# Linear attention and two MLPs on one core: who issues the weights' raw bits from unit 7 on

## The chip, the core and the metric

The kernel runs on one core of a Trainium2 chip. The metric is the device time of one execution in microseconds, as a median over several. TensorE does the matmuls, VectorE and ScalarE the elementwise work, GpSimd little else than memsets here. Any engine's instruction stream can start transfers between DRAM and SBUF; in this kernel nearly all are started by SyncE's (SP). Whatever stream starts them, they are carried out by the core's 16 DMA engines.

## The reference, cut to what matters

```python
def _attn_ref(q, k, v):            # 4 batches, 8 heads, 576 positions, 64 wide
    q_s = softmax(q, axis=-1)      # over the 64
    k_s = softmax(k, axis=2)       # over the 576
    kv = np.einsum('bhsd,bhse->bhde', k_s, v)
    return np.einsum('bhsd,bhde->bhse', q_s, kv)

x = attn_out.transpose(0, 2, 1, 3).reshape(2304, 512)
# first MLP: w_in 512 x 2048, w_out 2048 x 512
r = np.maximum(x @ w_in, 0.0)
x = (s * (r * r) + b) @ w_out
# second MLP, same sizes
h = x @ w_in2
out = (h * np.tanh(softplus(h))) @ w_out2
```

The two softmaxes and softplus are written out in the reference; they are shortened here. The weights of both MLPs reach the kernel as 64-bit floats.

## The kernel before, in words

**Stages.** Attention and the first MLP run interleaved in a loop of 80 steps: 5 chunks of tokens (512, 256, 512, 512, 512), each with 16 blocks of 128 hidden columns. Step n computes h of step n + 2 (`emit_h`, w_in times x), its activation (`emit_relu2`: ScalarE's Relu L222 and Square L223, a cast to a high part gh, and VectorE's low part gl, L175), and y of step n (`emit_y`, w_out times g). Every product is done in three passes of high and low parts (L185). The second MLP follows from about 470 us and is not touched.

**The first MLP's weights** come in 17 units. Units 0 and 1 hold one block of w_in, units 2 to 15 block f of w_in and block f - 2 of w_out, unit 16 the last two blocks of w_out. A block's raw bits are one transfer of 512 KB (`load_raw`, L116 for w_in, L121 for w_out); `load_w` issues a unit's two. They are turned into 32-bit floats by ScalarE's Abs (L133) and four passes on VectorE (L141, L145, L150, L155), and split into a high part (ScalarE, L164) and a low part (VectorE, L175), which take the place of the raw bits in the unit's slot.

**Slots.** Each unit has a slot of its own in SBUF, but some slots hold attention's data first: those of units 8 to 11 chunk 0's q of head pairs 0 to 3 (later also ke and km of batch 0), those of units 12 to 15 k, v and the block-diagonal kv of batch 0 (`kvb0` to `kvb3`, with `bd` in it). A raw load into such a slot waits until its last reader is done. For units 12 to 15 that is `kv_lo` of head pair 0 to 3 (VectorE's kvl, L175), which runs in chunk 1's part of the table below. The q of chunk 0 is loaded from ScalarE's stream; k, v and later q from SP's. Batches 1 to 3 share one buffer for k (`kb`) and one for v (`vb`), so each head pair's load waits for the one before to be used (k by VectorE's ke, L443; v by TensorE's kv, L487).

**Order.** A table (`at`, `run`) says in which step each load, conversion or attention stage is recorded. Raw bits of units 0 to 6 are recorded ahead of the loop (`early`), those of unit u from 7 on at the end of step u - 7; its high and low parts at step u - 3. What each engine then executes is decided by a scheduler, which simulates the recorded program and reorders each engine's instructions. So a different issuer for a transfer gives other orders on other engines as well. In the names below, `raw0_7` is the raw tile of unit 7, `t0_7` its converted copy, `w0_7` its high and low parts, `km1_0` the maximum of k for batch 1 and head pair 0, and `gl12` the low part of the activation of step 12.

The lines that decide which units the change touches:

```python
    for i in range(NU):
        u, s = (0, i), i - 3
        ...
        if s >= 4:
            at(s - 4, "load", load_w, *u)
        else:
            early.append((s, u))
```

Of the kernel before, what the change touches and what calls it, by code (L numbers as in the profile page):

```python
# [17 lines left out]
P = 128  # L18
# [9 lines left out]
def kernel(  # L28
# [21 lines left out]
    nc = tc.nc  # L50
    B, H, S, D = q.shape
    NT, DM = out.shape
# [56 lines left out]
    def slot(i, name, dt=F32):  # L109
        wp = next(pool for _, pool, last in wps if i <= last)  # L110
        return wp.tile([P, (2 if i < 2 else 4) * DM], dt, tag=f"w{i}", name=name)

    def load_raw(ph, z, f, part):
        src = srcs[ph, z].bitcast(I32)
        if z == "wi":
            nc.sync.dma_start(  # L116
                out=part.rearrange("p (k f) -> p k f", k=NK),
                in_=src[:, 2 * f * P:2 * (f + 1) * P].rearrange("(k p) f -> p k f", p=P),
            )
        else:  # L120
            nc.sync.dma_start(out=part, in_=src[f * P:(f + 1) * P, :])  # L121

    def load_w(ph, u):
        raw = slot(u, f"raw{ph}_{u}", I32)
        for i, (z, f) in enumerate(UNITS[u]):
            load_raw(ph, z, f, raw[:, 2 * i * DM:2 * (i + 1) * DM])
        w_raw[ph, u] = raw[:, 0:2 * len(UNITS[u]) * DM].rearrange("p (n w) -> p n w", w=2)

    def conv_abs(ph, u):
# [125 lines left out]
    def prep_load(z, i, pool):  # L255
        r = [pool.tile([P, 2 * DM], I32, tag="t", name=f"r{j}_{z}{i}") for j in range(2)]
        for j in range(2):
            load_raw(1, z, i + j * NF // 2, r[j])
        t, s = (pool.tile([P, 2 * DM], F32, tag="t", name=f"{a}_{z}{i}") for a in "ts")
        prep[z, i] = (r, t, s)  # L260
# [329 lines left out]
    def at(slot, what, fn, *args):  # L590
        todo.setdefault((slot, what), []).append((fn, args))
# [6 lines left out]
    for c in range(1, NC):  # L598
        wide = CHUNKS[c - 1] == CM
        for hp in range(NP):  # L600
            s = (c - 1) * NF + 3 * hp - (c > 1)
# [24 lines left out]
    for i in range(NU):  # L626
        u, s = (0, i), i - 3
        if s > 0:
            at(s - 1, "abs", conv_abs, *u)
            at(s - 1, "bits", conv_bits, u)  # L630
        if s >= 0:
            at(s, "hi", conv_hi, *u)
            at(s, "lo", conv_lo, *u)
        if s >= 4:
            at(s - 4, "load", load_w, *u)
        else:
            early.append((s, u))
    early.sort()
# [12 lines left out]
    for i in range(NF // 2):  # L651
        s = (17, 24, 31, 35, 39, 43, 47, 51)[i]
# [4 lines left out]
        s = (55, 59, 62, 63, 66, 67, 70, 71)[i]  # L657
# [7 lines left out]
    for hp in range(NP):  # L665
# [4 lines left out]
        if hp:  # L670
            v_load(0, hp - 1)
    load_w(*early[0][1])
    v_load(0, NP - 1)
    bds.append(ap.tile([P, P], F32, name="bd"))
# [3 lines left out]
    for _, u in early[1:4]:  # L678
        load_w(*u)
# [66 lines left out]
    for n in range(NS):  # L746
        ph, c, f = steps[n]
# [180 lines left out]
```

## Time and profile before

| | us |
|---|---|
| median of 3 runs | 857.91 |
| lowest and highest of them | 857.65, 861.57 |
| the profiled execution's own time | 858.7 |
| its span in the profile | 856.9 |
| TensorE, matmuls busy | 824.0 |
| VectorE busy | 630.5 |
| ScalarE busy | 495.9 |
| GpSimd busy | 3.7 |

The span runs from the first instruction to the last; the 1.8 us that the execution takes beyond it lie around it. The mean granted clock of TensorE was 0.994 of its full speed. Busy times of engines overlap one another, so they don't add up to the span. The times of rows come from the one profiled execution; the median comes from the others.

### The profile page before, as it was taken

How to read it: one execution, taken by the hardware profiler on the slowest of the kernel's cores; microseconds unless marked ns; L12 is line 12 of the kernel's file. 1: busy time of each engine (PE TensorE's matmuls, PEld its weight loads, DVE VectorE, ACT ScalarE, POOL GpSimd, SP SyncE). 2: the span in 40 equal slices, each digit the busy share in tenths (PEclk: the TensorE clock that was granted, in tenths of full speed). 3: DMA queues.
4: the chain of work that ended last, by engine and by line, in shares of the span. 5: the costliest groups of instructions: out<-in, count | busy, mean ns of one | idle time of the engine just before them, and what ended most of it. 6: DMA issues, size and time to landing. Idle time of an engine off the chain costs nothing.

```text
span 856.9 us, 14204 instructions
## 1 busy us (share of the span) xinstructions
PE 824.0 (96%) x5060; PEld 739.0 (86%) x5060; DVE 630.5 (74%) x1190; ACT 495.9 (58%) x1109; POOL 3.7 (0%) x26
## 2 busy tenths in 40 slices
PE   6798998999899999999999999999999999999998
PEld 4377877998678888888888699999999999999998
DVE  6999876576665657778685868776877858878764
ACT  7777675587666666646655744455444447244542
POOL 1000000000000000000000000000000000000000
PEclk9999999999999999999999999999999999999999
DMA  8992231566666314455797497888887888888882
GB/s 232 310 328 66 81 92 52 155 202 173 195 205 185 113 44 134 167 194 175 267 333 259 157 357 253 268 266 266 304 278 250 279 259 307 288 251 265 256 266 80
DMA packets 130150, 184.44 MB, mean 215 GB/s; under 512 B 43552, under 2 KB 94240, under 8 KB 130080
## 3 DMA queue, kind: packets, MB, share of 16 engines
q1 hardware_dynamic: 128992, 182.49, 66.4%
q10 hardware_dynamic: 1088, 1.05, 0.4%
q8 instruction: 40, 0.66, 0.3%
q14 instruction: 30, 0.25, 0.1%
HBM read 140.51 MB, written 42.99 MB: 214 GB/s over the span
## 4 chain that ended last, share of the span: by engine, by line
PE 73%; DVE 11%; DMA 9%; ACT 3%; SPq 2%; issue 2%; DVEq 0%; ACTq 0%
PE p L185 37%; PE y L185 17%; PE h L185 16%; DMA kb<-in_k_dram 2%; DMA raw<-in_moe_w_out_dram 2%; DMA xf<-yd 2%; DVE t L155 2%; DVE t L150 1%; PE x L185 1%; DVE xo L175 1%; DVE gl L175 1%; DVE w L175 1%; DVE t L288 1%; DMA r_wo<-in_moe_w_out_dram 1%; ACT xf L726 1%
## 5 line engine op out<-in xcount | busy, mean ns | idle before, releaser
L185 PE MATMUL h<-xh,w 128*128 128x512 f32 (+1 forms) x640 | 199.4, 376 | 10.1 <-ACT w L164 5.2
L185 PE MATMUL y<-gh,w 128*128 128x512 f32 (+1 forms) x640 | 196.0, 371 | 2.7 <-ACT gh L178 2.6
L185 PE MATMUL p<-ring,op 128*128 128x256 f32 x1512 | 183.0, 283 | 0.5 <-DVE op L175 0.3
L185 PEld LDWEIGHTS p<-ring,op 128*128 128x128 f32 x1512 | 182.4, 192 | 0.9 <-DVE op L175 0.9
L185 PE MATMUL p<-xo,ring 128*128 128x384 f32 x1008 | 175.9, 334 | 0.0
L185 PEld LDWEIGHTS p<-xo,ring 128*128 128x128 f32 x1008 | 174.6, 188 | 0.1
L185 PEld LDWEIGHTS h<-xh,w 128*128 128x128 f32 x640 | 118.0, 190 | 33.5 <-ACT w L164 6.0
L185 PEld LDWEIGHTS y<-gh,w 128*128 128x128 f32 x640 | 117.0, 189 | 23.0 <-ACT gh L178 3.7
L185 PE MATMUL y<-gl,w 128*128 128x512 f32 (+1 forms) x320 | 119.1, 375 | 6.0 <-DVE gl L175 5.9
L185 PE MATMUL h<-xl,w 128*128 128x512 f32 (+1 forms) x320 | 120.1, 376 | 0.0
L820 ACT ACTIVATE g<-g 128x384 f32<-128x384 f32 x96 | 50.5, 526 | 111.2 <-DVE g L288 111.1
L178 ACT CAST op<-g 128x384 fp32r<-128x384 f32 x144 | 72.8, 512 | 46.5 <-PE p L185 45.7
L175 DVE TENSOR_TENSOR op<-g,op 128x384 fp32r<-128x384 f32 x144 | 79.1, 555 | 24.2 <-ACT op L178 24.0
L175 DVE TENSOR_TENSOR gl<-r,gh 128x512 fp32r<-128x512 f32 (+1 forms) x80 | 50.7, 634 | 48.1 <-ACT gh L178 48.1
L288 DVE TENSOR_TENSOR u<-u,p 128x384 f32<-128x384 f32 (+1 forms) x117 | 57.4, 500 | 29.7 <-PE p L185 29.3
L185 PEld LDWEIGHTS y<-gl,w 128*128 128x128 f32 x320 | 60.6, 189 | 19.1 <-DVE gl L175 9.2
L222 ACT ACTIVATE r<-h 128x512 f32<-128x512 f32 (+1 forms) x80 | 44.2, 553 | 45.9 <-DVE gl L175 24.2
L185 PEld LDWEIGHTS h<-xl,w 128*128 128x128 f32 x320 | 60.9, 190 | 10.7 <-DVE xl L175 0.6
L288 DVE TENSOR_TENSOR g<-u,p 128x384 f32<-128x384 f32 x96 | 53.2, 554 | 15.1 <-PE p L185 11.8
L452 ACT ACTIVATE q<-q,qm 128x64 f32<-128x64 f32 x144 | 48.1, 337 | 12.9 <-DVE qm L433 12.7
L223 ACT ACTIVATE r<-r 128x512 f32<-128x512 f32 (+1 forms) x80 | 47.1, 588 | 1.6
L178 ACT CAST gh<-r 128x512 fp32r<-128x512 f32 (+1 forms) x80 | 46.0, 575 | 1.4
(127 smaller groups left out, 825.6 us busy)
## 6 DMA issues: line engine op xcount, KB each, us to landing
ring<-wo_d SPq DMA_DIRECT2D x84, 512.0 KB, 4.7
ring<-wi_d SPq DMA_DIRECT2D x72, 512.0 KB, 4.8
raw<-in_moe_w_in_dram SPq DMA_DIRECT2D x16, 512.0 KB, 5.9
raw<-in_moe_w_out_dram SPq DMA_DIRECT2D x16, 512.0 KB, 7.1
r_wi<-in_moe_w_in_dram SPq DMA_DIRECT2D x16, 512.0 KB, 5.7
wi_d<-r_wi SPq DMA_DIRECT2D x16, 512.0 KB, 3.0
r_wo<-in_moe_w_out_dram SPq DMA_DIRECT2D x16, 512.0 KB, 5.9
wo_d<-r_wo SPq DMA_DIRECT2D x16, 512.0 KB, 3.0
```

The source lines that it names most:

```text
L150: nc.vector.scalar_tensor_tensor(out=w_t[u], in0=w_raw[u][:, :, 1], scalar=-0x40000000, in1=w_t[u], op0=ALU.bitwise_and, op1=ALU.bitwise_or,)
L155: nc.vector.scalar_tensor_tensor(out=w_t[u], in0=w_raw[u][:, :, 0], scalar=29, in1=w_t[u], op0=ALU.logical_shift_right, op1=ALU.bitwise_or,)
L175: eng.tensor_tensor(out=lo, in0=src, in1=hi.bitcast(F32), op=ALU.subtract)
L178: nc.scalar.copy(out=hi, in_=src)
L185: mm = nc.tensor.matmul(out=ps, lhsT=x, rhs=y, start=start, stop=stop)
L222: nc.scalar.activation(out=r, in_=h_ps.pop(m), func=AF.Relu)
L223: nc.scalar.activation(out=r, in_=r, func=AF.Square)
L288: nc.vector.tensor_tensor(out=out, in0=a, in1=b, op=op)
L452: nc.scalar.activation(out=t[:, i // rq, i % rq], in_=t[:, i // rq, i % rq], func=AF.Exp, bias=mx[:, i], accum_out=sm[:, i])
L726: nc.scalar.activation(out=t, in_=t, func=AF.Identity, bias=bsum[:, kk:kk + 1])
L820: nc.scalar.activation(out=t, in_=t, func=AF.Mish)
```

## The change

`load_raw` and `load_w` are told which engine's stream to issue on, with SP's as the default. The loop's table passes GpSimd's for units 7 to 16: 20 transfers. Units 0 to 6 and all loads of attention and of the second MLP stay where they were.

```diff
--- before.py
+++ after.py
@@ -110,20 +110,20 @@
         wp = next(pool for _, pool, last in wps if i <= last)
         return wp.tile([P, (2 if i < 2 else 4) * DM], dt, tag=f"w{i}", name=name)
 
-    def load_raw(ph, z, f, part):
+    def load_raw(ph, z, f, part, eng=nc.sync):
         src = srcs[ph, z].bitcast(I32)
         if z == "wi":
-            nc.sync.dma_start(
+            eng.dma_start(
                 out=part.rearrange("p (k f) -> p k f", k=NK),
                 in_=src[:, 2 * f * P:2 * (f + 1) * P].rearrange("(k p) f -> p k f", p=P),
             )
         else:
-            nc.sync.dma_start(out=part, in_=src[f * P:(f + 1) * P, :])
-
-    def load_w(ph, u):
+            eng.dma_start(out=part, in_=src[f * P:(f + 1) * P, :])
+
+    def load_w(ph, u, eng=nc.sync):
         raw = slot(u, f"raw{ph}_{u}", I32)
         for i, (z, f) in enumerate(UNITS[u]):
-            load_raw(ph, z, f, raw[:, 2 * i * DM:2 * (i + 1) * DM])
+            load_raw(ph, z, f, raw[:, 2 * i * DM:2 * (i + 1) * DM], eng)
         w_raw[ph, u] = raw[:, 0:2 * len(UNITS[u]) * DM].rearrange("p (n w) -> p n w", w=2)
 
     def conv_abs(ph, u):
@@ -632,7 +632,7 @@
             at(s, "hi", conv_hi, *u)
             at(s, "lo", conv_lo, *u)
         if s >= 4:
-            at(s - 4, "load", load_w, *u)
+            at(s - 4, "load", load_w, *u, nc.gpsimd)
         else:
             early.append((s, u))
     early.sort()
```

Since the order of the engines' streams is the scheduler's, three places are shown where it differs.

The first is GpSimd's stream in the first microseconds, as a piece of the difference (a + is a row that is only in the changed kernel). The memsets prepare attention's tiles: `kb` and `vb` of the later batches, `kvb1` to `kvb3` of batch 0.

```order
 L354 MEMSET vb_116 128x10
 L677 MEMSET kb_115 64x2x64
+L116 DMA raw0_7_554<-in_moe_w_in_dram 128x4x256
+L121 DMA raw0_7_554<-in_moe_w_out_dram 128x1024
+L121 DMA raw0_16_1158<-in_moe_w_out_dram 128x1024 x2
 L355 MEMSET kvb1_130 64x130
 L355 MEMSET kvb2_142 64x130
 L355 MEMSET kvb3_154 64x130
 L355 MEMSET vb_116 64x130
+L116 DMA raw0_8_611<-in_moe_w_in_dram 128x4x256
+L121 DMA raw0_8_611<-in_moe_w_out_dram 128x1024
+L116 DMA raw0_9_663<-in_moe_w_in_dram 128x4x256
```

The loads of units 7 and 16 now stand among the memsets, ahead of four of them; units 8 and 9 follow, then 12, 10, 11, 13, 14 and 15. On SP's stream these 20 rows are gone.

The second place is VectorE's stream where unit 2 is converted. `xl0_0_3` is the low part of chunk 0's last x block, `t0_3` to `t0_5` belong to units 3 to 5, and `qs1_0` and `q1_0` to chunk 1's q. Before:

```order
L155 SCALAR_TENSOR_TENSOR t0_2_438<-raw0_2_180,t0_2_438 128x1024
L463 TENSOR_SCALAR qs1_0_558<-qs1_0_558 128x4
L150 SCALAR_TENSOR_TENSOR t0_3_447<-raw0_3_183,t0_3_447 128x1024
L141 TENSOR_SCALAR t0_4_493<-t0_4_493 128x1024
L464 RECIPROCAL qs1_0_558<-qs1_0_558 128x4
L141 TENSOR_SCALAR t0_5_563<-t0_5_563 128x1024
L175 TENSOR_TENSOR xl0_0_3_417<-x0_3_414,xh0_0_3_416 128x512
L425 TENSOR_REDUCE km1_0_523<-km1_0_525 128x1
L155 SCALAR_TENSOR_TENSOR t0_3_447<-raw0_3_183,t0_3_447 128x1024
L145 TENSOR_SCALAR t0_4_493<-t0_4_493 128x1024
L467 TENSOR_TENSOR q1_0_190<-q1_0_190,qs1_0_558 128x2x2x64
L175 TENSOR_TENSOR w0_2_444<-t0_2_438,w0_2_444 128x1024
```

In the changed kernel, from the same first low part of x on:

```order
L175 TENSOR_TENSOR xl0_0_3_417<-x0_3_414,xh0_0_3_416 128x512
L150 SCALAR_TENSOR_TENSOR t0_2_438<-raw0_2_180,t0_2_438 128x1024
L410 TENSOR_TENSOR km1_0_523<-kb_115 128x2x2x64
L141 TENSOR_SCALAR t0_3_447<-t0_3_447 128x1024
L155 SCALAR_TENSOR_TENSOR t0_2_438<-raw0_2_180,t0_2_438 128x1024
L425 TENSOR_REDUCE km1_0_523<-km1_0_525 128x1
L145 TENSOR_SCALAR t0_3_447<-t0_3_447 128x1024
L175 TENSOR_TENSOR gl0_480<-r0_481,gh0_479 128x512
L427 TENSOR_SCALAR km1_0_523<-ident_90,km1_0_523 128x128
L150 SCALAR_TENSOR_TENSOR t0_3_447<-raw0_3_183,t0_3_447 128x1024
L175 TENSOR_TENSOR w0_2_444<-t0_2_438,w0_2_444 128x1024
```

In the changed kernel unit 2's last two passes (L150 and L155) stand behind that low part of x, with the first rows of `km1_0` (L410, L425, L427, whose input is batch 1's k) and the first gl among them; rows of units 4 and 5 that stood ahead of unit 2's low part (the last row of both) stand behind it.

The third place is VectorE's stream where `kvl0_3` is made, the last reader of the slot of unit 15. `gl12`, `gl13` and `gl14` are low parts of activations, `qtl1_2` that of chunk 1's transposed q, `rs1_2` sums of batch 1. Before:

```order
L175 TENSOR_TENSOR w0_14_1225<-t0_14_1169,w0_14_1225 128x1024
L433 TENSOR_REDUCE qm2_0_1466<-q2_0_1382 128x8
L175 TENSOR_TENSOR kvl1_2_1125<-bd_173,kvh1_2_1124 128x128
L175 TENSOR_TENSOR kvl0_3_1253<-kvb3_154,kvh0_3_1252 128x128
L175 TENSOR_TENSOR gl12_1192<-r12_1193,gh12_1191 128x512
L425 TENSOR_REDUCE km1_3_1131<-km1_3_1133 128x1
L427 TENSOR_SCALAR km1_3_1131<-ident_90,km1_3_1131 128x128
```

In the changed kernel:

```order
L175 TENSOR_TENSOR w0_14_1225<-t0_14_1169,w0_14_1225 128x1024
L512 TENSOR_SCALAR rs1_2_1119<-kv1_2_1085 128x1
L515 RECIPROCAL rs1_2_1119<-rs1_2_1119 128x1
L175 TENSOR_TENSOR gl13_1246<-r13_1247,gh13_1245 128x512
L175 TENSOR_TENSOR qtl1_2_1128<-qt1_2_1096,qth1_2_1127 128x256
L175 TENSOR_TENSOR kvl1_2_1125<-bd_173,kvh1_2_1124 128x128
L175 TENSOR_TENSOR kvl0_3_1253<-kvb3_154,kvh0_3_1252 128x128
L425 TENSOR_REDUCE km1_3_1131<-km1_3_1133 128x1
L427 TENSOR_SCALAR km1_3_1131<-ident_90,km1_3_1131 128x128
L175 TENSOR_TENSOR gl14_1305<-r14_1306,gh14_1304 128x512
```

Before, `kvl0_3` stands ahead of `gl12`; in the changed kernel it stands behind `gl13`, which depends on h of step 13.

## Rows read from the trace of the kernel before

**Rows 1.** The page: span, and part 1, busy time by engine
```profile
span 856.9 us, 14204 instructions
...
PE 824.0 (96%) x5060; PEld 739.0 (86%) x5060; DVE 630.5 (74%) x1190; ACT 495.9 (58%) x1109; POOL 3.7 (0%) x26
```

**Rows 2.** TensorE's waits, whole run: us in total, times, longest us
```profile
PE y L185 <- DVE gl L175: 5.9, 7, 1.9
PE h L185 <- ACT w L164: 5.2, 3, 3.7
...
PE km L419 <- DVE km L410: 1.1, 1, 1.1
...
PE km L428 <- DVE km L427: 0.9, 1, 0.9
```

**Rows 3.** Busy us by stretch: PE, PEld, DVE, ACT, POOL; then clock, DMA, GB/s
```profile
10.00:15.00 5.00, 3.96 (x32) 2.88 (x32) 4.72 (x15) 4.76 (x23) 0.00 (x0) 1.00 0.76 169
...
20.00:25.00 5.00, 4.95 (x39) 2.41 (x40) 4.83 (x13) 4.67 (x11) 0.00 (x0) 1.00 1.06 369
25.00:30.00 5.00, 3.50 (x29) 1.76 (x24) 4.96 (x13) 4.70 (x8) 0.00 (x0) 1.00 0.63 177
40.00:100.00 60.00, 54.80 (x278) 42.78 (x277) 60.00 (x87) 43.99 (x82) 0.00 (x0) 1.00 0.51 164
```

**Rows 4.** The chain in order of time, 100 to 135 us
```profile
114.33 1.06 ACT w L164
...
117.23 0.41 DVE kvl L175 x2
...
118.12 4.71 DMA raw<-in_moe_w_out_dram
...
130.83 1.05 ACT w L164
...
131.93 1.22 PE h L185 x2
```

**Rows 5.** TensorE's timeline, 115 to 133 us
```profile
117.88 0.47 PE L185 MATMUL h<-xh,w 128*128 128x512 f32 x1
...
127.06 0.80 PE L487 MATMUL kv<-vb,ke 128*64 128x65 f32 x20
127.80 0.44 PE L496 MATMUL qt<-ident,q 128*128 128x128 f32 x2
```

**Rows 6.** GpSimd's timeline, 0 to 15 us
```profile
4.08 0.20 POOL L677 MEMSET kb<- 64x128 f32 x1
```

**Rows 7.** Timelines: TensorE's from 12.5 us, SP's from 35 us
```profile
12.88 1.35 PE L487 MATMUL kv<-kvb,q 128*64 128x65 f32 x20
...
36.02 0.60 SPq L116 DMA_DIRECT2D raw<-in_moe_w_in_dram  x1
...
40.92 0.46 SPq L116 DMA_DIRECT2D raw<-in_moe_w_in_dram  x1
```

**Rows 8.** Transfers: the chain; the raw tiles; the page's DMA issues (KB, us)
```profile
20.85 8.40 DMA kb<-in_k_dram
...
DMA to landing us min/median/max: 3.9/6.5/12.1
...
raw<-in_moe_w_out_dram SPq DMA_DIRECT2D x16, 512.0 KB, 7.1
```

**Rows 9.** VectorE's conversion: its timeline, and the chain
```profile
41.55 1.22 DVE L175 TENSOR_TENSOR w<-t,w 128x1024 fp32r<-128x1024 f32 x1
...
50.38 0.60 DVE t L141
50.98 1.14 DVE t L155
```

**Rows 10.** The page, part 5: ScalarE's costliest groups of MLP1's activation
```profile
L222 ACT ACTIVATE r<-h 128x512 f32<-128x512 f32 (+1 forms) x80 | 44.2, 553 | 45.9 <-DVE gl L175 24.2
...
L223 ACT ACTIVATE r<-r 128x512 f32<-128x512 f32 (+1 forms) x80 | 47.1, 588 | 1.6
L178 ACT CAST gh<-r 128x512 fp32r<-128x512 f32 (+1 forms) x80 | 46.0, 575 | 1.4
```

## Prediction

> **What bounds the kernel now.** I read the page first. TensorE is busy for 824.0 of 856.9 us [rows 1], so a change can win at most some 33 us, and only where TensorE waits. The list of TensorE's waits says where. For gl, the low part of an MLP activation that VectorE makes, it waits 5.9 us in seven places; for ScalarE's high part of a weight unit 5.2 us in three places, of which one is 3.7 us; for km of attention's second batch 1.1 and 0.9 us [rows 2]. The table by stretches says why. VectorE is busy for all 60 us from 40 to 100: it converts the weights, and no work on it can be late there without TensorE feeling it. The 16 DMA engines are full early (a share of 1.06 from 20 to 25 us); 10 to 15 us with 0.76 and 25 to 30 us with 0.63 have room [rows 3]. So the start (0 to 45 us) hangs on transfers, the middle on VectorE, and from about 130 us TensorE itself is the bound.
>
> The 3.7 us is one chain, and it is the one that the change touches. kv_lo of head pair 3 (second of the two kvl at 117.23) frees the slot that raw bits of unit 15 go into; SP then issues them, they land at 122.8, ScalarE's Abs and VectorE's bits follow, and the high part ends at 131.88; the h matmul of unit 15 begins at 131.93 [rows 4]. From the kvl's end (117.64) to that matmul are 14.3 us. TensorE had ended h of unit 13 at 118.35, and its own work was done at 128.24 [rows 5]: 9.9 us of work against 13.6 us of chain, so 3.7 us of waiting.
>
> **What the change moves.** Twenty transfers of 512 KB (units 7 to 16, some 10 MB) leave SP's queue for GpSimd's. Nothing is added or removed in computation. Four consequences, each costed alone.
>
> 1. SP's time. SP loses 20 issues of 0.4 to 0.6 us, and its waits for slots of units 8 to 15. Behind those waits stood k, v and q of chunk 1. k has one buffer, though, and its next load still waits for VectorE's ke; TensorE's waits that name this km are 1.1 and 0.9 us, each in one place [rows 2]. I cost the gain at 0, bounds 0 and -2.0.
>
> 2. The start. GpSimd's last memset ahead of its first new issue begins at 4.08 us [rows 6], so units 7 and 16 (2.1 MB) are asked for then and not from 36 us on; unit 8 follows when head pair 0's q slot is free (its kv matmuls end at 14.2 us) and not at 40.92; unit 9 behind it [rows 7]. SP needs the same engines for attention's first k and v, raw of units 0 to 3 and k of chunk 1. 1.05 MB at the 369 GB/s of the busiest early stretch takes 2.85 us [rows 3]. Units 7 and 16 cost 5.7 us, less the 1.2 us of room from 10 to 15 us; 8 costs 2.85 and 9 about half, less its room: some 9 us in front of k of chunk 1, which landed at 29.25 [rows 8], so at about 38. On VectorE's new order this k (km of head pair 0) stands ahead of the second half of unit 2 (rows of the order above). From 38.2: km 0.33, unit 3's first step 0.6, unit 2's last step 1.13, then 0.4 + 0.6 + 0.6 + 0.2 + 1.13 for the rows between, and unit 2's low part 1.13 by [rows 9] for 1024 elements (0.60 for tensor_scalar, 1.13 for the others) and by size for the smaller ones: 44.3. Before, that low part ended at 42.8. That is 1.5 us late, with no delay added for the order of the queues; since VectorE has no idle time behind it until 100 us, I carry 2 us to TensorE. Lower bound: all of this hidden. Then the new order, which puts some 3 us of units 3 to 5 behind unit 2's low part, gives 3 us back. Upper bound: the whole 11.4 us of units 7, 16, 8 and 9 land on the path, less 3.5 us of gl waits that would be absorbed: 8. Range -3 to +8, taken +2, since the nearest row (1.06) says that the engines have little room.
>
> 3. Unit 15. The order decides here. Before, the two kvl stand ahead of gl of step 12; in the changed kernel they stand behind gl of step 13. That gl needs h of unit 13, and so ReLU 0.55, Square 0.59 and cast 0.58 [rows 10]; ahead of the kvl come five small ones of ScalarE (cast of q, two copies into bd, two casts), at most 0.57 each by the same rows and by their size an estimate of 2.0 together, and 0.4 for the pair itself [rows 4]. It ends some 4.1 us behind the end of h of unit 13; gl lies under ScalarE's part. Before, it was 0.7 us ahead of it. TensorE's work between that end and h of unit 15 grows too, because kv and q's transpose of head pair 2 (0.80 and 0.44, as pair 3's [rows 5]), its x products and km's transposes now stand there: to the 9.9 us of before come 1.2 and an estimate of 1.8 for the twelve small matmuls: 12.9 us. So 4.1 + 14.3 - 12.9 = 5.5 us of waiting against 3.7: +1.8 if GpSimd's transfer lands as fast as SP's did (4.7 us from the second issue). No transfer of before goes by GpSimd. Bounds: as SP's here, 0; or the slowest of the 32 raw transfers, 12.1 us from issue to landing, 7.4 us more [rows 8]. I take 1.3, half the way to the 7.1 us that is the median of the w_out ones. Term: +3.1, bounds +1.8 and +9.2.
>
> 4. Units 7 to 14 have cover: unit 14's high part ended at 115.4 [rows 4], when TensorE still had h of unit 13 to end and y of step 11 ahead of it [rows 5], and its kvl now stands ahead of gl of step 9, as before. The four memsets that now queue behind four of GpSimd's issues are needed first by kv of head pair 1, which comes behind pair 0's end at 14.2 us [rows 7]: four issues of 2.5 us would still be hidden. Cost 0.
>
> Against its own execution of 858.7 us: 858.7 + 2 + 3.1 = 863.8. That execution lies 0.8 us above the median of 857.91, so **863 us**.
>
> A rule of the Trainium skill speaks against the change. The page "SBUF — State Buffer", section "SBUF: two separate sides", says that a DMA issued from GpSimd has its descriptors written by GpSimd's cores, and that they are locked out while VectorE runs an operation in a 2-port mode. VectorE's rows show an f32 tensor_scalar on 1024 elements at 0.60 us beside 1.13 for the two-input forms [rows 9], which fits such a mode; that GpSimd is held up no run here shows. By the rule the sum would go up by a share of a VectorE operation for each issue on the path, to the fourth rival below.
>
> **The rivals.**
> - *Hidden start, same end* (within 0.5%): the early loads find enough room and unit 15 waits only 1.8 us more. 857.9 - 1 + 1.8 = 858.7; with the start at +1, 860.7. For it: 37% of the engines' time from 25 to 30 us is free. Against: the full engines ahead of it.
> - *Faster*: the rewritten order. gl stands ahead of conversion work in many more places, and the 5.9 us of gl waits go [rows 2], and the start gives its 3 us; with unit 15 at +1.8 that is 857.9 - 5.9 - 3 + 1.8 = 850.8. It decides if k of chunk 1 lands by about 34 us, so that unit 2's low part ends by 40.
> - *Much slower*: GpSimd's issues are slow among VectorE's work. If each of unit 15's two transfers takes 2.5 us longer, and the early ones push the whole 11.4 us in front of units 0 to 3, it is 857.9 + 8 + 3 + 3 = about 872. By the page above, this is where the lock would lead; for it speaks VectorE's 60 of 60 us [rows 3].
> - *No effect at all* can be left out: the order shows every one of the twenty on GpSimd's queue.
>
> By another page of the Trainium skill, "DMA: Bandwidth & Descriptors", section "Issuing engines are not separate DMA queues", issuing from more engines saves only the issue time, as all transfers share the 16 engines. That is the first consequence at its bound and the second at its cost; by it alone the time would be 860 and more.
>
> **How the numbers follow.** 863 as summed (861.5 to 867): 0.38. Much slower (867 to 875): 0.16. Within 4.3 us of 857.9, which is 0.5% and about what a measurement of this kernel can tell from no change: 0.33, of which most lies above 857. Faster by more: 0.13. The sum stands just outside the 0.5%, so part of its own range falls to "same"; I give faster 0.14, same 0.34, slower 0.52. The range that leaves out no more than 2 in 10 is 854 to 871: it takes in the hidden start and most of the gl gain below, and the start's upper bound with unit 15 at +3 above.
>
> **What would show it.** In the changed kernel's profile: raw of units 7 and 16 landing before 20 us; k of chunk 1 landing near 38; VectorE idle in short pieces between 20 and 40 us; y of step 0 starting near 45 and not 42.8; a wait of TensorE of 5 us or more (in one or two pieces, at kv of head pair 3 and at h of unit 15) around 132 us. I am wrong if VectorE shows no idle time before 45 us (then the start is free), if the kvl of head pair 3 runs before h of unit 13 ends (then unit 15 is no loss), or if the waits for gl are gone between 55 and 85 us (then it is faster).

## The result and the profile after

The changed kernel takes 872.25 us (median of 4 runs, 871.35 to 872.44) and the kernel before 859.28 us beside it (857.65 to 861.57): 13.0 us more, a ratio of 1.0147 with a 95% interval of 1.0118 to 1.0176. The forecast was 863, range 854 to 871: slower, as said, but more than twice as much so, and 1.3 us outside the range.

The page of the profiled execution answers to [rows 1]:

```profile
span 870.3 us, 14225 instructions
...
PE 827.6 (95%) x5060; PEld 743.1 (85%) x5060; DVE 630.5 (72%) x1190; ACT 496.0 (57%) x1109; POOL 16.4 (2%) x46
```

The span grew by 13.4 us. TensorE's busy time grew by 3.6 us with the same 5060 matmuls, so 9.8 us are idle time. Where they lie, the table by stretches shows: the stretch and its length; busy time (and rows) of TensorE, its weight loads, VectorE, ScalarE and GpSimd; then granted clock, DMA share and GB/s. First the kernel before, then the changed one:

```profile
0.00:40.00 40.00, 27.53 (x165) 17.35 (x166) 31.03 (x71) 30.55 (x104) 3.70 (x26) 0.96 0.91 265
40.00:60.00 20.00, 17.41 (x90) 12.95 (x88) 20.00 (x30) 15.61 (x29) 0.00 (x0) 1.00 1.06 368
60.00:140.00 80.00, 73.70 (x387) 59.26 (x388) 67.71 (x107) 55.70 (x124) 0.00 (x0) 0.98 0.29 79
140.00:200.00 60.00, 58.86 (x517) 55.89 (x516) 38.03 (x84) 41.77 (x118) 0.00 (x0) 1.00 0.58 171
200.00:300.00 100.00, 95.50 (x522) 77.63 (x521) 62.96 (x125) 65.39 (x174) 0.00 (x0) 0.98 0.55 166
```

```profile
0.00:40.00 40.00, 22.04 (x145) 14.10 (x145) 21.25 (x54) 23.02 (x88) 12.55 (x40) 0.95 1.01 318
40.00:60.00 20.00, 14.45 (x48) 11.34 (x49) 15.02 (x24) 12.77 (x24) 0.00 (x0) 0.68 0.87 273
60.00:140.00 80.00, 76.14 (x397) 61.38 (x395) 68.37 (x106) 54.62 (x104) 3.84 (x6) 0.98 0.23 66
140.00:200.00 60.00, 53.33 (x414) 48.75 (x415) 38.18 (x77) 39.12 (x116) 0.00 (x0) 0.94 0.45 131
200.00:300.00 100.00, 98.30 (x606) 81.86 (x605) 66.39 (x136) 71.77 (x203) 0.00 (x0) 1.00 0.58 175
```

Subtracting busy time from each stretch, idle time is 5.5 us more from 0 to 40 us, 3.0 more from 40 to 60, 3.1 more from 60 to 200 (2.4 less up to 140, 5.5 more behind it), and 2.8 less from 200 to 300; the rest, to the end, is 1.1 more. So the start carries 8.5 of the 9.8 us. In the second stretch the mean granted clock is 0.68 of full speed where it was 1.00, after TensorE's longest wait (7.17 us, up to 43.59), so part of the stretch ran at the lower of the two levels, 1.2 GHz (0.50 from 40 to 48 us). h's matmuls kept TensorE busy for 0.36 us each in it (9.97 us for 28), before for 0.25 (9.36 for 38): for 28 of them that is 3.1 us, most of the 3.6 that were added to the busy time.

What the start waits for is shown by ScalarE's Abs of units 1, 2 and 3 on its timeline (in brackets the idle time ahead and what ended it):

```profile
33.30 0.66 ACT L133 ACTIVATE t<-raw 128x512 f32<-128x512 f32 x1 [2.21 <-DMA raw<-in_moe_w_in_dram]
...
41.91 1.12 ACT L133 ACTIVATE t<-raw 128x1024 f32<-128x1024 f32 x1 [6.67 <-DMA raw<-in_moe_w_out_dram]
...
45.45 1.19 ACT L133 ACTIVATE t<-raw 128x1024 f32<-128x1024 f32 x1 [1.31 <-DMA raw<-in_moe_w_out_dram]
```

Before, these three began at 23.54, 24.73 and 27.57 us. All three wait for SP's transfers, which the change did not touch. The chain of the changed kernel has unit 2's second transfer in it:

```profile
24.12 17.70 DMA raw<-in_moe_w_out_dram
...
42.92 0.62 ACT w L164
...
43.59 5.93 PE h L185 x13
```

Before, SP had issued it at 17.29 us. GpSimd's timeline up to 35 us says what was beside it:

```profile
4.22 0.90 POOL L116 DMA_DIRECT2D raw<-in_moe_w_in_dram  x1
5.11 1.57 POOL L121 DMA_DIRECT2D raw<-in_moe_w_out_dram  x3
...
16.74 0.76 POOL L116 DMA_DIRECT2D raw<-in_moe_w_in_dram  x1 [9.40 <-DVE q L410]
17.50 0.53 POOL L121 DMA_DIRECT2D raw<-in_moe_w_out_dram  x1
20.97 0.76 POOL L116 DMA_DIRECT2D raw<-in_moe_w_in_dram  x1 [2.94 <-issue]
...
22.74 0.76 POOL L116 DMA_DIRECT2D raw<-in_moe_w_in_dram  x1 [0.49 <-PE kv L487]
...
24.78 0.76 POOL L116 DMA_DIRECT2D raw<-in_moe_w_in_dram  x1 [0.77 <-issue]
...
31.81 0.76 POOL L116 DMA_DIRECT2D raw<-in_moe_w_in_dram  x1 [5.75 <-ACT w L164]
```

That is units 7 and 16, then 8, 9, 12, 10 and 11: 12 transfers by 26.1 us and 14 by 33.1, some 7.3 MB. In 40 us the engines moved 318 GB/s where they had moved 265 (12.7 MB, not 10.6). So 2.1 MB of the 7.3 were extra and about 5.2 MB pushed out others: at the 376 GB/s of the busiest five microseconds (35 to 40 us) that is, as an estimate, 14 us of transfers. From 20 to 35 us the table of DMA queues shows it directly (packets, MB, share of the 16 engines; then issues, KB each, median us to landing). `q0` is GpSimd's queue (10.49 MB in the whole run, its 20 loads), `q1` SP's:

```profile
q0 software_dynamic: 995, 3.62, 67.1%
q1 hardware_dynamic: 2641, 1.65, 38.4%
...
raw<-in_moe_w_in_dram POOLq DMA_DIRECT2D x4, 512.0 KB, 9.8
raw<-in_moe_w_out_dram POOLq DMA_DIRECT2D x4, 512.0 KB, 10.8
raw<-in_moe_w_in_dram SPq DMA_DIRECT2D x3, 512.0 KB, 17.8
raw<-in_moe_w_out_dram SPq DMA_DIRECT2D x2, 512.0 KB, 18.7
```

In the kernel before, the same stretch had `q1` alone:

```profile
q1 hardware_dynamic: 3884, 4.39, 89.1%
```

In the raw tiles' view the issue itself tells the same (ns, least, median, most):

```profile
L121 POOL DMA_DIRECT2D raw<-in_moe_w_out_dram x11: 528/528/531, 5.1 to 134.0; - x11
L116 POOL DMA_DIRECT2D raw<-in_moe_w_in_dram x9: 761/761/895, 4.2 to 133.3; - x9
...
L121 SPq DMA_DIRECT2D raw<-in_moe_w_out_dram x5: 502/599/6203, 24.1 to 48.8; - x5
...
DMA to landing us min/median/max: 4.1/7.5/19.8
```

GpSimd's issues take 0.53 or 0.76 us here (the first 0.90), and over the whole run its transfers land in 6.1 and 7.4 us (medians for w_in and w_out; SP's were 5.9 and 7.1 before). It is SP's that suffer most: one of its issues took 6.2 us, and the slowest raw transfer, SP's for unit 3, 19.8 us against 12.1 [rows 8].

### The profile page after: what moved, and what is told of

Same layout as the page of the kernel before. It is cut to its first block, busy times and chain, and to the rows that moved or that the text cites. A ratio compares the mean times of both kernels' runs of the same rounds, so it can differ in the third digit from the quotient of the medians.

```text
span 870.3 us, 14225 instructions
## 1 busy us (share of the span) xinstructions
PE 827.6 (95%) x5060; PEld 743.1 (85%) x5060; DVE 630.5 (72%) x1190; ACT 496.0 (57%) x1109; POOL 16.4 (2%) x46
## 3 DMA queue, kind: packets, MB, share of 16 engines
q0 software_dynamic: 2880, 10.49, 3.5%
## 4 chain that ended last, share of the span: by engine, by line
PE 77%; DVE 8%; DMA 8%; ACT 3%; SPq 2%; issue 2%; POOL 0%; DVEq 0%; ACTq 0%; POOLq 0%
PE p L185 36%; PE h L185 19%; PE y L185 19%; DMA raw<-in_moe_w_out_dram 2%; DMA xf<-yd 2%; PE x L185 1%; DMA kvb<-in_v_dram 1%; DMA kb<-in_k_dram 1%; DVE xo L175 1%; DVE op L175 1%; DMA q<-in_q_dram 1%; DVE t L288 1%; ACT q L452 1%; PE kv L487 1%; PE qt L496 1%
## 5 line engine op out<-in xcount | busy, mean ns | idle before, releaser
L185 PE MATMUL h<-xh,w 128*128 128x512 f32 (+1 forms) x640 | 200.3, 378 | 13.6 <-ACT w L164 12.7
L185 PEld LDWEIGHTS h<-xh,w 128*128 128x128 f32 x640 | 118.4, 191 | 36.3 <-ACT w L164 14.3
L185 PEld LDWEIGHTS y<-gl,w 128*128 128x128 f32 x320 | 61.6, 192 | 13.5 <-DVE gl L175 3.3
L185 PEld LDWEIGHTS h<-xl,w 128*128 128x128 f32 x320 | 61.4, 192 | 10.6 <-DVE xl L175 0.7
```

The costliest lines, as they stand in the source:

```text
L185: mm = nc.tensor.matmul(out=ps, lhsT=x, rhs=y, start=start, stop=stop)
```

## The experiments

Theory A: GpSimd's loads start early and crowd out, on the shared DMA engines, what is needed sooner. Rivals: it is GpSimd's own way of issuing (B), or the late slot of unit 15 (C). Two more came up on the way, on the gain of the versions without early loads: SP's queue set free (D), or the order and the moment of the loads, whoever issues (E).

Each version gets an order of its own from the scheduler, and the versions ran on several chips. The ratio is to the kernel before, run beside each on the same chip (its medians there are 858.99 to 860.36 us). Beside the median the table gives two places in each version's profile, found by counting twelve matmuls a step on TensorE's timeline: the start of h of step 3, which the transfers of the start set, and the start of y of step 68, near the end of the first MLP.

| version | early transfers on the second queue, by 35 us | h, step 3 | y, step 68 | median | ratio (95% interval) |
|---|---|---|---|---|---|
| before | 0 | 48.45 | 435.93 | 859.28 | 1 |
| changed | 14 | 59.86 | 447.84 | 872.25 | 1.0147 (1.0118 to 1.0176) |
| e1, held until unit 6 has landed | 0 | 51.08 | 429.27 | 847.05 | 0.9857 (0.9824 to 0.9889) |
| e2, only 7 and 16 | 4 | 49.52 | 427.07 | 849.78 | 0.9888 (0.9855 to 0.9922) |
| e3, 8 to 15 | 10 | 52.17 | 445.98 | 869.91 | 1.0110 (1.0070 to 1.0151) |
| e4, before and 12 unread | 12 | 53.87 | 448.25 | 873.97 | 1.0173 (1.0125 to 1.0222) |
| e5, changed, kvl early | 17 | 67.25 | 449.38 | 871.65 | 1.0122 (1.0099 to 1.0145) |
| e6, only 8 to 11 | 8 | 52.74 | 438.74 | 860.21 | 0.9994 (0.9977 to 1.0011) |
| e7, changed, ScalarE issues | 12 | 60.58 | 448.07 | 875.23 | 1.0169 (1.0139 to 1.0199) |
| e8, held until unit 3 has landed | 8, from 28.9 on | 51.01 | 447.48 | 868.91 | 1.0096 (1.0077 to 1.0115) |
| e9, before and 4 unread | 4 | 49.86 | 436.42 | 861.37 | 1.0012 (0.9993 to 1.0031) |
| e10, only 12 to 15 | 2 | 50.77 | 437.73 | 859.16 | 0.9998 (0.9969 to 1.0027) |
| e11, e1 with kvl early | 0 | 47.74 | 426.79 | 849.71 | 0.9894 (0.9854 to 0.9934) |
| e12, 7 and 16 free, 8 to 15 held | 4 | 48.46 | 430.32 | 849.79 | 0.9882 (0.9861 to 0.9903) |
| e13, e1 with SP as issuer | 0 | 48.88 | 429.11 | 849.71 | 0.9909 (0.9876 to 0.9942) |
| e14, e1 again | 0 | 51.76 | 429.45 | 849.47 | 0.9884 (0.9865 to 0.9903) |

**Hold the loads back (e1).** GpSimd copies two values of unit 6's raw bits into a small tile, and from there into each raw slot, so its transfers wait for unit 6. The computation is unchanged.

```diff
+    gate = const.tile([P, 2], I32, name="gate")
...
         raw = slot(u, f"raw{ph}_{u}", I32)
+        if u >= 7:
+            nc.gpsimd.tensor_copy(out=raw.rearrange("p (h w) -> p h w", h=2)[:, :, 0], in_=gate)
...
+    nc.gpsimd.tensor_copy(out=gate, in_=w_raw[0, 6].rearrange("p (h n) w -> p h n w", h=2)[:, :, 0, 0])
     for hp in range(NP):
```

> The changed kernel, but GpSimd copies one column of the raw bits of unit 6 into a small tile and from there into each raw slot of units 7 to 16, so that none of its 20 transfers starts before unit 6 has landed. Theory A (early bytes: the start is late because GpSimd asks for 12 transfers of 512 KB ahead of 33 us, which share the DMA engines with attention's first loads and units 1 to 3): h of step 3 starts within 2 us of the 48.45 us of the kernel before, not at 59.9, and the time is 857 to 863 us. Theory B (GpSimd's issue is slow, or held up while VectorE works): nothing is mended, 868 us or more. Theory C (unit 15's slot comes free late): the wait near unit 15 stays, about 3 us, and the start as in A: 861 to 864 us.

It took 847.05 us: not only is the loss gone, it is 10 us below A's range, and so faster than the kernel before by more than the early loads explain (D and E, below). GpSimd's first raw transfer starts at 43.68 us, step 3 is 2.6 us late, and the stretches from 0 to 40 and 40 to 60 us have TensorE busy for 26.48 and 17.55 us, nearly the 27.53 and 17.41 of before. Still all 20 are GpSimd's, so theory B falls. The wait for high parts is 1.2 us in the whole run, so C's 3 us are not there. (The expectations say 12 transfers ahead of 33 us; the timeline has 14.)

**Take the units apart (e2, e3, e6, e10).** One line of the changed kernel's table decides who issues which unit:

```diff
-            at(s - 4, "load", load_w, *u, nc.gpsimd)
+            at(s - 4, "load", load_w, *u, nc.gpsimd if i in (7, 16) else nc.sync)
```

e3 has `i not in (7, 16)`, e6 `8 <= i <= 11` and e10 `12 <= i <= 15`.

> Only units 7 and 16 on GpSimd (4 transfers, asked for from about 4 us on), 8 to 15 stay on SP. Theory A: a third of the early bytes, all of them in front of attention's first k and v: h of step 0 about 4 us late (31 us and not 26.5), h of step 3 some 4 to 6 us late, 862 to 866 us. Theory B: the few issues of GpSimd meet no VectorE work at 4 us, 858 to 860 us. Theory C: no loss, since unit 15 is issued by SP: 858 to 860 us.

> Units 8 to 15 on GpSimd, 7 and 16 back on SP. Theory A: the early bytes are 8 transfers from about 16 us on instead of 12 from 4 us on: h of step 0 on time (26.5 us), h of step 3 some 6 to 8 us late, 865 to 869 us. Theory B: nearly as the changed kernel, 870 to 873 us. Theory C: the whole loss is unit 15's, 870 to 873 us.

> Only units 8 to 11 on GpSimd, which wait for the slots of chunk 0's q. Theory A (bytes that are asked for between 16 and 26 us, where units 1 to 3 are loaded, do the harm; those at 4 us do none, as the run with units 7 and 16 alone showed): h of step 1 some 5 us late or more, 862 to 870 us, near the 869.9 of the run with units 8 to 15. Theory C: no loss, 858 to 861 us.

> Only units 12 to 15 on GpSimd. Theory A: one unit (12) is early, at about 22 us, so the start is 0 to 2 us late, and SP no longer waits for the slots of units 12 to 15 ahead of attention's k: 852 to 861 us. Theory C (unit 15, late through GpSimd, costs time of its own): 861 to 865 us, with a wait of 5 us or more ahead of h of step 15.

e2 went against all three: h of step 0 is 2.6 us late (29.02 us), step 3 only 1.1, and the time is 849.78. Transfers at 4 us are nearly free when they are the only early ones. e3 has the early transfers from 14.8 us on: step 3 is 3.7 us late, less than the 6 to 8 expected, and the time is 869.91, between A's range (to 869) and that of B and C (from 870), so it decides nothing. Its start explains only part: y of step 28 is 3.6 us late and y of step 36 is 9.7, with a single wait for VectorE's km between them, which the kernel before does not have in this length:

```profile
224.59 0.80 PE L428 MATMUL km<-km,ones 128*128 128x128 f32 x2 [4.77 <-DVE km L427]
```

e8 (below) has the same wait, 4.00 us, and e1 has none of this length; whether it comes of a late start or of the order, no run separates.

The two parts of the early crowd do not simply add up. At unit 2's Abs they do: 4.6 us late in e2 (29.28), 11.6 in e3 (36.31) and 17.2 in the changed kernel. At step 3 they are 1.1, 3.7 and 11.4. So, as far as versions with orders of their own can tell, units 7 and 16 cost next to nothing alone, but beside the others they are part of the loss.

e6 is 8.7 us late at step 1, as A had it, 4.3 at step 3 and 2.8 at step 68, while its median equals that of before. By its time it lies in C's range (858 to 861) and not in A's (862 or more), so a late start of 4 us can be lost among what an order gives or takes. e10 is as before, within A's range; C's 861 to 865 us did not come.

**Bytes alone (e4, e9).** The kernel before, with unread transfers on GpSimd into the slots of units 7 and 16, in three groups (e4) or one (e9); `load_raw` takes the issuer as in the changed kernel:

```diff
+    for j in range(3):
+        for u in (7, 16):
+            d = slot(u, f"d{u}_{j}", I32)
+            for i, (z, f) in enumerate(UNITS[u]):
+                load_raw(0, z, f, d[:, 2 * i * DM:2 * (i + 1) * DM], nc.gpsimd)
     for _, u in early[1:4]:
         load_w(*u)
```

> The kernel before with all its loads on SP, and on top 12 transfers of 512 KB that GpSimd issues early and nobody reads: units 7 and 16, three times over, into the slots of these two units, four at a time, each group when the one ahead has landed. Theory A: bytes alone make the start late, h of step 3 some 8 to 12 us late, 866 to 873 us. Theory B and C: 858 to 861 us, since what the computation needs is still issued by SP and in the old sequence.

> The kernel before, with four transfers of 512 KB on top that GpSimd issues at about 4 us into the slots of units 7 and 16 and that nobody reads. It prices the early share of the changed kernel alone, without the relief later that moving units 7 and 16 gives. Theory A as the prediction had it (5.7 us of engine time less 1.2 us of room): h of step 3 about 4 us late, 861 to 864 us. If bytes at 4 us find room, as the run with units 7 and 16 on GpSimd suggests: h of step 3 within 1.5 us of the 48.45 us of the kernel before, 857 to 861 us.

e4 took 873.97 us, as long as the changed kernel, although SP issues all that is read. Its delay comes in two parts: 5.4 us at step 3, and by step 8 it is 14.8 us (98.06 against 83.24), while SP still loads the raw bits of the later units: the DMA share from 60 to 80 us is 0.96, with TensorE busy for 12.69 of the next 20 us. The changed kernel has no such second part (12.7 us at step 8): e4 adds 6.3 MB, where the change only moves its bytes forward. That the two times agree is luck; what e4 shows is that bytes alone make the start late. e9 is at 861.37, a ratio whose interval holds 1, and 1.4 us late at step 3: alone, four transfers at 4 us cost next to nothing, where the prediction's sum had 4.5 us for them (5.7 less 1.2).

**Another issuer (e7).** The changed kernel with `nc.scalar` for `nc.gpsimd` in the table.

> The changed kernel with ScalarE's stream as the issuer of units 7 to 16 in place of GpSimd's. Theory A: the early transfers are there as well as soon as a slot is free, so the start is late by 5 to 12 us whoever issues, 865 to 875 us. Theory B (it is GpSimd's own way of issuing): the loss is gone, 857 to 861 us.

It took 875.23 us, with step 3 at 60.58 against the changed kernel's 59.86. The loss is not GpSimd's. ScalarE's own work waits behind its issues too (TensorE waited 10.3 us for its copies into `kvb`, L518), so its size is not a clean price.

**Where the gate stands (e8).** As e1, with the raw bits of unit 3 for those of unit 6.

> As the run that was held back until unit 6 had landed, but until unit 3 has landed, which frees GpSimd's queue some 10 us earlier, while k of chunk 1 and units 4 to 6 are still to come. Theory A: units 1 to 3 are on time, units 4 to 6 share with 7 to 9, so between the two: 848 to 856 us.

This missed: 868.91 us and not 848 to 856. Eight transfers start between 28.9 and 34.5 us; step 3 is on time (51.01), step 4 is 11.3 us late (66.62 against 55.32). TensorE's timeline shows whom they pushed:

```profile
58.14 1.35 PE L490 MATMUL kv<-vb,ke 128*64 128x65 f32 x18 [3.08 <-DMA vb<-in_v_dram]
63.04 0.79 PE L188 MATMUL y<-gl,w 128*128 128x512 f32 x1 [2.93 <-DVE gl L178]
```

v of batch 1 is late now, and with it what follows. So it is not units 1 to 3 alone that need protection, but whatever is needed next. The time does not price this delay, though: at y of step 28 only 3.8 us of it are left, and 7 more come up to step 36, with the wait for km that e3 has too.

**Unit 15's slot (e5, e11).** The changed kernel (e5) and e1 (e11) with kvh and kvl of batch 0 recorded earlier:

```diff
-                at(s + o[2], "att1", kv_hi, 0, hp)
-                at(s + o[2], "att1", kv_lo, 0, hp)
+                at(hp // 2, "att1", kv_hi, 0, hp)
+                at(hp // 2, "att1", kv_lo, 0, hp)
```

> The changed kernel with the high and low parts of kv of batch 0 (kvh, kvl) recorded in steps 0 and 1 instead of 2, 5, 8 and 11, so that the slots of units 13 to 15 come free early. Theory C (unit 15's late slot costs some of the loss): the wait of 7.2 us at about 141 to 148 us is gone, 866 to 869 us. Theory A: units 13 to 15 are now also asked for early, 6 transfers more beside units 1 to 6, so the start is as late or later (h of step 3 at 60 us or more) and C's gain is used up: 870 to 875 us.

> The run held back until unit 6 had landed, with kvh and kvl of batch 0 recorded in steps 0 and 1, so that units 13 to 15 load early too, behind the gate. Theory C: TensorE's wait for unit 15 goes for good, 842 to 846 us. Theory A: unit 15 had cover already (1.2 us of waiting for high parts in all), and three units more in the stretch from 45 to 80 us compete with attention's k, q and v: 847 to 852 us.

e5 is at 871.65, and its start at 67.25 for step 3: units 13 to 15 now join the crowd. (The 7.2 us wait that its expectation puts near unit 15 is the one at the start, up to 43.59 us; near unit 15 there are two of 4.79 and 1.99.) At step 12 its y is 21.0 us late (145.28 against 124.25), at step 68 only 13.5. e11 did not gain on e1 either. Removing the wait brings nothing, but neither run shows it alone.

**Both (e12).** e1 with the gate for units 8 to 15 only.

> Units 7 and 16 free to start at 4 us, units 8 to 15 held back until unit 6 has landed. If the gains of the two runs have one source (the crowd of transfers between 36 and 60 us thinned out), 845 to 849 us; if they add, 838 to 842 us; if the early four cost the start something, 849 to 853 us.

At 849.79 the gains do not add. The time lies in the range for an early cost and 0.8 us above that for one source; step 3 is on time (48.46), and the spread does not tell the two apart.

**SP again (e13, e14).** e1 with `nc.sync` in the table: GpSimd makes the small copies, SP issues all 20. By a line-by-line difference of VectorE's 1190 rows in the traces (buffer numbers left out), its order differs from e1's in 66 lines and from that of the kernel before in 226.

> The run held back until unit 6 had landed, but with all 20 transfers on SP, as in the kernel before, and GpSimd only making the small copies ahead of them. The orders of VectorE and ScalarE are nearly those of the run held back on GpSimd. Theory D (SP's queue: attention's k, v and q of chunk 1 wait behind raw loads and their slots, and a second queue frees them): the gain is gone, 857 to 862 us. Theory E (the gain is in the rewritten orders and in the moment of the loads, whoever issues): 846 to 850 us.

> The run held back until unit 6 had landed, on GpSimd, once more on the chip of the run with SP, so that the two are compared on one chip: 846 to 849 us.

849.71 and 849.47 us on one chip: theory D falls. A second queue is worth nothing here beyond the spread, and the 9 to 10 us that e1 gains on the kernel before come with what e13 shares with it: the other order and the moment of the loads, which no run separates (E). TensorE's stretches in e13, beside those of before above:

```profile
40.00:60.00 20.00, 17.30 (x91) 13.04 (x89) 20.00 (x30) 15.09 (x26) 3.90 (x8) 1.00 0.90 336
60.00:140.00 80.00, 75.99 (x408) 61.21 (x409) 68.86 (x112) 59.32 (x134) 1.66 (x3) 1.00 0.31 88
140.00:200.00 60.00, 59.40 (x522) 56.12 (x521) 39.13 (x86) 42.01 (x120) 0.00 (x0) 1.00 0.58 176
200.00:300.00 100.00, 96.53 (x528) 78.71 (x527) 66.37 (x128) 70.57 (x190) 0.00 (x0) 1.00 0.51 163
```

From 60 to 300 us it idles for 8.1 us where the kernel before idles for 11.9. That is 3.9 of the 9.6 us of span. The other 6 are busy time (818.0 against 824.0, summed over all stretches); where they come from stays open.

## Why the prediction was off, point by point

**The start (step 2) is the step that failed.** It carried +2 us, with bounds of -3 and +8. Measured: 8.5 us of idle time and 3.1 us of busy time at the lower clock, 11.6 in all, and 11.4 us of delay at step 3. y of step 0 began at 53.11 us, not near 45. The mechanism was the right one (e4 shows it with bytes alone, e1 shows that it goes when the bytes wait), but four things were wrong in the sum.

- It counted units 7, 16, 8 and half of 9. The slots of units 12, 10 and 11 came free at 23 to 32 us as well, and GpSimd's order shows all of them next in line. I stopped reading that order at the piece that is shown ahead of the prediction.
- It put those bytes in front of k of chunk 1 and so priced unit 2's last pass on VectorE. That k landed at 46.3 and 46.5 us, not at 38, but what lay closest was the raw bits of units 1 to 3 themselves: unit 2's Abs began 17.2 us late (41.91 against 24.73). Of these, 6.8 us are SP's late issue of its second transfer (24.12 against 17.29); the transfer then took 17.7 us, where SP's raw transfers of this stretch had taken 6.0 and 6.9 (medians). VectorE is busy for 15.02 of the 20 us up to 60, where it had been for all 20.
- It had "no delay added for the order of the queues". From 20 to 35 us GpSimd's queue moved 3.62 MB and SP's, which had what was needed first, 1.65; why the shares are so unequal, no run shows.
- It had no term for the clock after a wait of 7 us.

The part that was counted first, units 7 and 16 at 4.5 us, costs next to nothing alone (e9: ratio 1.0012): a delay of 2.6 to 4.1 us at step 0 (e2, e9) is 1.1 to 1.4 at step 3. Beside the others it is not free: without it the delay at step 3 is 3.7 us (e3), with it 11.4. That the upper bound, too, had 11.4 us before the gl waits came off is luck: it had 8 transfers, and 14 came.

**SP's time (step 1) at 0: right** as far as e13 and e14 go, where all 20 loads are held back and leave SP's queue for 0.2 us; in the changed kernel itself no run shows it alone.

**Unit 15 (step 3) at +3.1: the size and most of its terms were right, but the price is given back.** The kvl of head pair 3 ran at 132.36 us, behind gl of step 13 (130.82), and ended at 132.64. Unit 15's high part ended at 148.78 and h of unit 15 began at 148.83: 16.2 us for the chain that I had at 15.6 (14.3 and 1.3). GpSimd's second transfer took 5.7 us from its issue to the Abs (134.04 to 139.73) against SP's 4.7, near the 1.3 us more that I had put on it (half the way to the median of 7.1 is 1.2, a slip of 0.1). TensorE's two waits, 4.79 us at kv and 1.99 at x, sum to 6.8 us against 3.7: 3.1 us more, as is the idle time from 60 to 200 us. They do not stand at h, where I had expected one: kv waits for ke's exponential, which stands on ScalarE behind the Abs of units 15 and 16 and six rows of q's, and starts at 143.76. h could not have begun sooner than its high part either way; which of the two holds TensorE, no run separates. At h of step 14 the kernel is 11.1 us behind, at step 15 16.9, and at y of step 36 11.5 again: from 200 to 300 us the kernel before idles for 4.5 us and the changed one for 1.7, which gives 2.8 back. So little of it is left at the end; this is read from the two traces, and no run shows it alone.

**Units 7 to 14 (step 4) at 0: right.** TensorE's waits for high parts behind 60 us, 3.6 us in two places, stand before h of steps 4 and 6: units 4 and 6, SP's.

**The rivals.** The much slower case gave 872, and 872.25 came, but that is luck: of its parts only the early crowd is true. Its other part, GpSimd's issues held up among VectorE's work, is not: the changed kernel's 20 issues took 0.53 to 0.90 us, and e7 loses as much with another issuer. An issue is held up in other versions, by tenths of a microsecond: beside VectorE's tensor_scalar (L144 and L148 there, L141 and L145 here) it takes 0.92 and 0.98 us in e1 (48.21 and 52.43 us) for 0.76, and at most 0.97 in e8 (44.75) for 0.53. That fits the rule of the Trainium skill in "SBUF — State Buffer", "SBUF: two separate sides", that GpSimd is locked out of writing descriptors while VectorE runs a 2-port mode. With the loads held back, 20 issues from GpSimd or from SP give the same time (849.47 and 849.71 us), and the changed kernel's loss comes with ScalarE as issuer too (e7). That agrees with the Trainium skill's "DMA: Bandwidth & Descriptors", "Issuing engines are not separate DMA queues": the shared engines decide, and another issuer saves only the time of issuing. The 860 and more that I gave by it had the right sign. The faster rival's waits for gl did shrink, from 5.9 to 2.2 us, and the late start outweighed it. Its size came in other versions, but not always for its reason: e2 waits 1.8 us for gl, e13 5.9 as before.

**A missing term.** For the order the prediction had 3 us at the start and, in the faster rival, the 5.9 us of gl. e1, e13 and e2 show that a rewritten order with no late start, together with other moments for the loads, is worth 9 to 13 us, as much as the whole lower half of the range or more.

## What to carry to other kernels

A transfer that waits in a queue behind others is also being held back: giving it a queue of its own lets it start as soon as its buffer is free, beside transfers that are needed sooner, and then the sooner ones are late. Count every transfer of the freed queue that can start in the stretch where the DMA engines are full, by following that queue's order against the times at which its buffers come free, and hold back what is needed later (a small copy from a tile that must land first will do it). Put the hold behind all that the full stretch needs: behind unit 3 it was too early (e8), behind unit 6 it was not (e1). Where a scheduler rewrites all orders, compare with a version that has nearly the same order before crediting a queue: here the kernel takes 849.5 us with the 20 held-back loads on GpSimd and 849.7 with them on SP.

## What was not expected of the hardware

An issue on SP took up to 6.2 us while another queue's transfers filled the engines (of these raw loads 2.3 at most before); GpSimd's never took more than 0.90 us in the changed kernel. Raw transfers issued from 20 to 35 us landed in 17.8 and 18.7 us (medians) when they were SP's and in 9.8 and 10.8 when they were GpSimd's. So the queue that issues what is needed first is slowed twice, in its transfers and in its issues.
